# Where unit 30 spreads its inverses: ahead of, or behind, a marker in SyncE's queue

## The chip, the cores and the metric

The kernel runs on one core of a Trainium2 chip. The metric is the device time of one execution in microseconds (us), as the median of several runs; lower is better.

## The reference

Multi-query attention with 32 heads and a gated feed-forward part are computed from the same 2048 x 512 input, and mixed row by row by a gate:

```
g = sigmoid((x * gate_w).sum(-1, keepdims=True))
q = (x @ wq) in 32 heads of 16;   k = x @ wk;   v = x @ wv
p = softmax(q k^T * 16 ** -0.5);  a = (p v, heads side by side) @ wo
b = (sigmoid(x @ w_gate) * (x @ w_up)) @ w_down
out = g * a + (1 - g) * b
```

All of it is float32. F is 1792.

## The kernel before

The queries stand in 4 blocks of 512 rows (b), the heads in 8 groups of 4, so attention has 32 units, u = 0 to 31. For each unit TensorE first makes scores to find each row's maximum (L1141, reduced by VectorE at L1143), then makes the scores again with the maxima taken off (L1150), ScalarE takes their exponentials (L1152, tiles `p`), and TensorE multiplies these by the values (L1008, "V" here: 4 matmuls for each of 16 chunks of keys). `v_aug` has a column of ones, so the sums of the softmax come out of the same matmuls. Between these stand the matmuls of the feed-forward part and of the output projection (`fill`, L1115). They use 64 of the 128 rows each, so two of them, or one and a score matmul, run side by side in the two halves.

A matmul pair of `fill` changes halves in the middle of a job: what half 0 has begun in a bank, half 1 goes on with. For this the kernel puts an empty instruction, a marker, in SyncE's queue (L1119). It waits for the last matmul of the first half, and the first matmul of the other half on that bank waits for the marker (`CROSS`, L1117).

SyncE also issues every DMA, all in one queue and in program order. So an instruction of SyncE that waits holds up all DMAs behind it.

What a unit needs at its end goes through these steps. `finish` (L1015) and `add_sums` (L1022) bring the values of the unit together in tile `ou`. `store` sends the sums to DRAM tile `sd` (L1030) and all of `ou` to `od` (L1031). `sums` reads the sums back in another shape into `rc` (L1036). `invert` takes the reciprocals on VectorE (L1045). `send_inverse` writes them to DRAM tile `rd` (L1049). `spread` reads `rd` back into `bc`, each row repeated over the 16 rows of its head (L1055). `divide` on GpSimd multiplies `vd` by `bc` (L1063) and splits the product into a high and a low part, tile `o` (L755 and L756). `o` is an operand of the output projection.

Units go by twos through `vd`, `bc` and `o`, with one exception. Unit 30, the last but one, does not wait for unit 31: its heads are put into both halves of `vd` and `bc`, so that its `spread` issues four DMAs, `bc`, `vd`, `bc`, `vd` (L1055, L1057, L1055, L1057). Its projection is a job of its own, "e" (matmuls `bank<-we,o`, 12 of them), which lies among the scores and values of unit 31. Unit 31 itself is finished by other code at the end of the kernel (L1177 to L1208).

The order of all work is fixed beforehand. TensorE's order is a string written out by hand (`ORDER`, one character a step). The steps of the other engines are put between by a small planner (`State`), which keeps an estimated time, in a unit of its own, for each engine: `self.now` for TensorE, `self.sp` for SyncE's queue, `self.dma` for transfers. An event is put on a list with an estimated time (`after`, L181) and is written into the program at the first step of TensorE whose estimated time is not earlier (`tick`, L280). `send` and `issue` (L169, L175) advance `self.sp` by the cost of issuing and return an estimate of when the data has landed. At the end each engine's instructions are chained in that program order. The estimates set only the order; on the chip semaphores decide when something runs.

Of the kernel before, what the change touches and what calls it, by code (L numbers as in the profile page):

```python
# [26 lines left out]
NU = NB * NG  # L27
# [30 lines left out]
ISSUE, SMALL, TEN_KB, LAST, SAFE, SURE = 185, 750, 20, 300, 300, 150  # L58
# [64 lines left out]
class State:  # L123
# [170 lines left out]
    def event(self, what, args):  # L294
        self.acts.append((what, *args))
        if what == "load_x":
            self.x_loaded[args[0]] = self.send(KC, 1024)
        elif what == "store_q":
            at = self.send(2, 512)
            self.q_ready[tuple(args)] = at  # L300
            self.ba_release(("query", *args), at)
        elif what == "send_max":
            self.after(self.issue(SEND_SQUARE, 16) + SAFE, "place_max", *args)
        elif what == "max_square":
            self.after(self.on("dve", self.now, SQUARE) + TAIL, "send_max", *args)
        elif what == "place_max":
            self.max_ready[args[0]] = self.issue(PLACE, 16) + 150
        elif what == "store":
            at = self.sums_free[args[0] % OU] = self.issue(470, 264) + SAFE
            self.after(at, "sums", *args)  # L310
        elif what == "sums":
            self.after(self.issue(430, 136) + 2 * SAFE, "invert", *args)
        elif what == "invert":
            self.after(self.on("dve", self.now, INVERSE), "send_inverse", *args)
        elif what == "send_inverse":
            self.after(self.send(1, 8) + SAFE, "spread", *args)
        elif what == "spread":
            u = args[0]
            at = self.issue(250, 128)
            if u % 2 or u == NU - 2:  # L320
                self.task(2, at + 2 * SAFE, "divide", u)
        elif what == "out":
            self.tile_free[self.tile_of[tuple(args)]] = self.send(1, 256)
# [933 lines left out]
```

## Time and profile before

| What | us |
|---|---|
| Median of 3 runs (1583.82 to 1584.93) | 1583.95 |
| The profiled execution, its own time | 1582.52 |
| Span of its profile, first to last instruction | 1580.7 |
| TensorE matmuls (PE) busy | 1567.2 (99%) |
| VectorE (DVE) busy | 1338.9 (85%) |
| ScalarE (ACT) busy | 1232.2 (78%) |
| GpSimd (POOL) busy | 803.8 (51%) |
| DMA, mean over the span | 65 GB/s |

PE is TensorE's matmuls, PEld its loading of weights, and SPq is SyncE's queue with its DMA issues. Times of single rows count from the start of the span. A row of the timeline gives the start, the duration, the engine, the line, the operation with output and inputs, how many instructions were merged into the row, and in brackets how long the engine stood idle before it and what ended that. Matmuls of the two halves overlap, so the busy times of single lines add up to more than the time that passes.

### The profile page before, as it was taken

The numbers are of one execution on the slowest core, as the hardware profiler recorded it, in microseconds if no ns is written. First come the engines' busy times: TensorE is split into PE (matmuls) and PEld (weight loads), VectorE is DVE, ScalarE is ACT, GpSimd is POOL, SyncE is SP. The second block draws the span as 40 slices with busy tenths as digits, with TensorE's granted clock in tenths as the row PEclk, the third lists the DMA queues.
The fourth block names the chain that finished last, engine by engine and source line by source line (L and its number), as shares of the span: only waits on it lengthen the run. The fifth ranks groups of instructions, "written<-read, shape, count | busy, mean of one in ns | idle before, by whom it ended". The sixth has DMA issues, their size and how long they took to land.

```text
span 1580.7 us, 33642 instructions
## 1 busy us (share of the span) xinstructions
PE 1567.2 (99%) x12910; PEld 1009.0 (64%) x12910; DVE 1338.9 (85%) x2277; ACT 1232.2 (78%) x2429; POOL 803.8 (51%) x727
## 2 busy tenths in 40 slices
PE   9999999999999999999999999999999999999997
PEld 7766666666666666666666666667675666656653
DVE  6899899988898888889798888888889888988841
ACT  4277878788788787878788777878878887878895
POOL 4353472655574164367475346275547517357351
PEclk9999999999999999999999999999999999999999
DMA  7421120222122121122122212021213202111011
GB/s 245 169 88 51 35 86 16 66 62 83 43 83 66 36 79 53 35 76 71 45 83 63 64 49 78 18 67 60 77 46 92 65 23 87 46 40 59 18 53 40
DMA packets 63076, 103.43 MB, mean 65 GB/s; under 512 B 24530, under 2 KB 24786, under 8 KB 62916
## 3 DMA queue, kind: packets, MB, share of 16 engines
q1 hardware_dynamic: 62916, 101.29, 20.5%
q8 instruction: 101, 1.65, 0.4%
q14 instruction: 59, 0.48, 0.1%
HBM read 79.51 MB, written 21.75 MB: 64 GB/s over the span
## 4 chain that ended last, share of the span: by engine, by line
PE 96%; DVE 1%; DMA 1%; SPq 1%; ACT 0%; issue 0%; POOL 0%; DVEq 0%; ACTq 0%; POOLq 0%
PE bank L1115 32%; PE bank L1008 29%; PE bank L1141 17%; PE bank L1150 16%; PE bank L853 2%; DVE mx L1143 1%; DMA vd<-od 0%; DMA wqr<-wq 0%; SPq L968 0%; DVE q L948 0%; DMA qs<-qd 0%; ACT x L780 0%; PE bank L1196 0%; DVE x L786 0%; SPq L765 0%
## 5 line engine op out<-in xcount | busy, mean ns | idle before, releaser
L1143 DVE TENSOR_REDUCE mx<-bank 128x1 f32<-128x512 f32 x2048 | 1253.7, 680 | 168.7 <-PE bank L1141 104.0
L1152 ACT ACTIVATE p<-bank 128x512 f32<-128x512 f32 x2048 | 1040.2, 664 | 10.9 <-PE bank L1150 7.7
L1150 PE MATMUL bank<-qs,ks 64*128 64x512 f32 x2048 | 723.7, 399 | 0.0
L1141 PE MATMUL bank<-ks,qs 64*128 64x512 f32 x2048 | 684.2, 404 | 0.5 <-DMA qs<-qd 0.5
L1008 PE MATMUL bank<-p,v_aug 128*32 128x512 f32 x4096 | 480.6, 597 | 0.0
L1141 PEld LDWEIGHTS bank<-ks,qs 64*128 64x128 f32 x2048 | 339.8, 184 | 138.7 <-issue 56.5
L1150 PEld LDWEIGHTS bank<-qs,ks 64*128 64x128 f32 x2048 | 359.6, 184 | 91.3 <-ACT p L1152 27.8
L1015 ACT COPY ou<-bank 128x512 f32<-128x512 f32 x205 | 125.0, 610 | 272.3 <-PE bank L1008 124.1
L1022 POOL TENSOR_TENSOR ou<-ou,ou 128x512 f32<-128x512 f32 x174 | 224.3, 1289 | 170.2 <-ACT ou L1015 167.7
L1115 PE MATMUL bank<-wd,hl 64*128 64x512 f32 x1344 | 272.7, 391 | 0.0
L1115 PE MATMUL bank<-x,wu 64*128 64x512 f32 x1344 | 271.3, 390 | 0.6 <-SPq L1119 0.4
L1008 PEld LDWEIGHTS bank<-p,v_aug 128*32 128x32 f32 x4096 | 113.1, 109 | 248.4 <-issue 220.5
L1115 PE MATMUL bank<-x,wg 64*128 64x512 f32 x1344 | 271.2, 391 | 0.0
L1115 PEld LDWEIGHTS bank<-wd,hl 64*128 64x128 f32 x1344 | 199.8, 184 | 20.6 <-issue 2.5
L1115 PEld LDWEIGHTS bank<-x,wg 64*128 64x128 f32 x1344 | 200.8, 184 | 17.5 <-issue 1.2
L1115 PEld LDWEIGHTS bank<-x,wu 64*128 64x128 f32 x1344 | 201.1, 184 | 17.0 <-issue 2.5
L1094 POOL TENSOR_TENSOR ba<-ba,pa_d 128x512 f32<-128x512 f32 x35 | 44.5, 1283 | 93.2 <-ACT pa_d L1091 93.1
L829 POOL CAST wg<-rg 128x1024 fp32r<-128x1024 f32 x27 | 28.0, 1039 | 123.8 <-PE bank L1115 63.9
L829 POOL CAST wu<-ru 128x1024 fp32r<-128x1024 f32 x27 | 28.1, 1040 | 95.8 <-PE bank L1115 93.2
L756 POOL TENSOR_TENSOR wd<-rd,wd 128x512 fp32r<-128x512 f32 x56 | 72.3, 1292 | 4.5
L756 POOL TENSOR_TENSOR hl<-h,hl 128x512 fp32r<-128x512 f32 x56 | 72.0, 1286 | 4.5
L1115 PE MATMUL bank<-wa,o 64*128 64x512 f32 x360 | 70.4, 391 | 0.0
(80 smaller groups left out, 747.2 us busy)
## 6 DMA issues: line engine op xcount, KB each, us to landing
rg<-wg SPq DMA_DIRECT2D x28, 512.0 KB
ru<-wu SPq DMA_DIRECT2D x28, 512.0 KB
rd<-wd SPq DMA_DIRECT2D x28, 512.0 KB
qs<-qd SPq DMA_DIRECT2D x192, 64.0 KB
qd<-q SPq DMA_DIRECT2D x32, 256.0 KB
od<-ou SPq DMA_DIRECT2D x31, 256.0 KB
xf<-x_in SPq DMA_DIRECT2D x16, 256.0 KB
vd<-od SPq DMA_DIRECT2D x32, 128.0 KB
```

The lines of the kernel that those rows point to most:

```text
L756: lo.tensor_tensor(hl[:, 1, :], raw, f32(hl[:, 0, :]), op=ALU.subtract)
L829: nc.gpsimd.tensor_copy(WS[item][:, 0, :], raw)
L853: nc.tensor.matmul(ps, w[:, p, part(kc)], X[b, kc][:, q, :], start=i == 0, stop=i == 3 * KC - 1)
L1008: nc.tensor.matmul(ps[32 * j:32 * j + 32, :], v_aug[:, c, :], PT.pop((u, c, j)), start=start, stop=stop)
L1015: nc.scalar.copy(to, ps)
L1022: nc.gpsimd.tensor_tensor(SUMS[u], SUMS[u], PARTS_OF[u].pop(0), op=ALU.add)
L1094: nc.gpsimd.tensor_tensor(BA[b, t], BA[b, t], PA[b, t].pop(0), op=ALU.add)
L1115: ins = nc.tensor.matmul(banks[i], l, r, start=start, stop=stop)
L1141: nc.tensor.matmul(banks[i], qs_t[u % 3][r, pr, part(qt)], ks[r, kb * 512:(kb + 1) * 512], start=True, stop=True)
L1143: nc.vector.tensor_reduce(MX[u][:, pr, h, qt, kb:kb + 1], banks[i], axis=AX.X, op=ALU.max)
L1150: nc.tensor.matmul(banks[i], ks[r, part(c)], qs_t[u % 3][r, pr, :], start=True, stop=True)
L1152: nc.scalar.activation(p, banks[i], AF.Exp, scale=0.25)
```

## The change

One event of the planner is due at another time. Before, `spread` was put on the list for the moment at which `send_inverse` is estimated to have landed, plus a margin (`SAFE`). Now, for unit 30 alone, it is put there for the moment at which SyncE is estimated to have issued `send_inverse`. The other units keep their order.

```diff
         elif what == "send_inverse":
-            self.after(self.send(1, 8) + SAFE, "spread", *args)
+            at = self.send(1, 8) + SAFE
+            self.after(self.sp if args[0] == NU - 2 else at, "spread", *args)
         elif what == "spread":
             u = args[0]
             at = self.issue(250, 128)
             if u % 2 or u == NU - 2:
                 self.task(2, at + 2 * SAFE, "divide", u)
```

The changed file has one line more, so lines behind it carry a number greater by one (L1055 is L1056 there). In the rows below the tiles of unit 30 are `sd_20058`, `od_20059`, `rc_20107`, `rd_20150`, `bc_20057` and `vd_20056`; a marker has no row of its own, and shows in the waits of the SyncE instruction behind it (`PE_49`) and of the TensorE matmul that needs it (`SP_sequencer_49`).

SyncE's queue from the sending of the sums of unit 30 to the end, before:

```order
L1030 DMA sd_20058<-ou_19636 4x512 [waits PE_49,DMAHW4_49,Pool_49]
L1031 DMA od_20059<-ou_19636 128x512
L1036 DMA rc_20107<-sd_20058 128x16 [waits DMAHW6_49,DMAHW4_49]
L1049 DMA rd_20150<-rc_20107 128x16 [waits DMAHW7_49,DVE_49]
L1055 DMA bc_20057<-rd_20150 64x1x512 [waits PE_49,DMAHW7_49,DMAHW0_49]
L1057 DMA vd_20056<-od_20059 64x1x512 [waits DMAHW5_49]
L1055 DMA bc_20057<-rd_20150 64x1x512 [waits DMAHW2_49]
L1057 DMA vd_20056<-od_20059 64x1x512 [waits DMAHW3_49]
L1207 DMA out<-ba_0_16676 128x512 [waits PE_49,DVE_49]
```

The same place now:

```order
L1031 DMA sd_20058<-ou_19636 4x512 [waits PE_49,DMAHW4_49,Pool_49]
L1032 DMA od_20059<-ou_19636 128x512
L1037 DMA rc_20107<-sd_20058 128x16 [waits DMAHW6_49,DMAHW4_49]
L1050 DMA rd_20150<-rc_20107 128x16 [waits DMAHW7_49,DVE_49]
L1056 DMA bc_20057<-rd_20150 64x1x512 [waits DMAHW7_49,DMAHW0_49]
L1058 DMA vd_20056<-od_20059 64x1x512 [waits DMAHW5_49]
L1056 DMA bc_20057<-rd_20150 64x1x512 [waits DMAHW2_49]
L1058 DMA vd_20056<-od_20059 64x1x512 [waits DMAHW3_49]
L1208 DMA out<-ba_0_16676 128x512 [waits PE_49,DVE_49]
```

The DMAs stand in the same order. What moved is a marker: before, the marker of the last "a" job's first half on bank 7 stood between `rd` and the first `bc`, and is the `PE_49` of that `bc`. Now it stands behind the four DMAs of `spread`, beside the marker of bank 2, which stood there already.

On TensorE the two matmuls that need these markers, on bank_79 (bank 7) and bank_74 (bank 2), stand among scores of unit 31, before:

```order
L1115 MATMUL bank_74<-wa_1_0_19890,o_19717 128x512
L1150 MATMUL bank_72<-qs_108,ks 128x512 [waits Activation_49]
L1115 MATMUL bank_79<-wa_0_0_19783,o_17409 128x512 [waits SP_sequencer_49]
L1150 MATMUL bank_76<-qs_108,ks 128x512 [waits Activation_49]
L1115 MATMUL bank_79<-wa_0_0_19783,o_17409 128x512
L1150 MATMUL bank_78<-qs_108,ks 128x512 [waits Activation_49]
L1115 MATMUL bank_79<-wa_0_0_19783,o_17409 128x512
L1150 MATMUL bank_75<-qs_108,ks 128x512 [waits Activation_49]
L1115 MATMUL bank_79<-wa_0_1_19786,o_18682 128x512
L1115 MATMUL bank_74<-wa_0_0_19783,o_17409 128x512 [waits SP_sequencer_49]
```

Nothing moved there: these rows and all others of TensorE, VectorE, ScalarE and GpSimd stand in the same order in the changed kernel. The first use of `o` of unit 30 (tile `o_20240`), 24 rows further on in TensorE's order, before:

```order
L1008 MATMUL bank_77<-p_8_1_1_20170,v_aug 32x512
L1150 MATMUL bank_73<-qs_108,ks 128x512 [waits Activation_49]
L1115 MATMUL bank_79<-we_0_0_19958,o_20240 128x512 [waits DVE_49,Pool_49]
L1115 MATMUL bank_72<-we_0_0_19958,o_20240 128x512 [waits Activation_49]
L1115 MATMUL bank_79<-we_0_0_19958,o_20240 128x512
L1115 MATMUL bank_72<-we_0_0_19958,o_20240 128x512
L1115 MATMUL bank_79<-we_0_0_19958,o_20240 128x512 [waits Pool_49]
L1150 MATMUL bank_76<-qs_108,ks 128x512 [waits Activation_49]
```

Here too the order is the same now, and so are the waits; only the numbers that tiles get in program order differ (`o_20240` is `o_20200`). The first of these five "e" matmuls waits for the high part of `o`, the fifth for the low part.

## The prediction

> **What bounds the kernel now.** I read the page first (engines, chain), then the chain in order of time near the end, then SyncE's waits and the timelines of SyncE, GpSimd, TensorE and ScalarE around unit 30's `spread`.
>
> ```profile
> PE 1567.2 (99%) x12910; PEld 1009.0 (64%) x12910; DVE 1338.9 (85%) x2277; ACT 1232.2 (78%) x2429; POOL 803.8 (51%) x727
> PE 96%; DVE 1%; DMA 1%; SPq 1%; ACT 0%; issue 0%; POOL 0%; DVEq 0%; ACTq 0%; POOLq 0%
> ```
>
> TensorE is busy for 99% of the span and carries 96% of the chain. Only where the chain leaves TensorE can the order of another queue be worth anything. Near the end it does:
>
> ```profile
> 1547.13 0.26 PE bank L1150
> 1547.47 0.07 issue
> 1547.60 0.57 SPq L1055
> 1548.16 0.05 issue
> 1548.22 0.55 SPq L1057
> 1548.81 0.51 SPq L1055
> 1549.36 6.18 DMA vd<-od
> 1555.60 0.09 issue
> 1555.69 1.27 POOL vd L1063
> ```
>
> Read from below: `divide` waited for the last of the four transfers of `spread`, that one for SyncE's issue, and the first issue (1547.60) for a matmul of TensorE that ended just before. A transfer between DRAM tiles and `bc` has no business waiting for a matmul; the waits of SyncE between 1530 and 1560 us tell what it was:
>
> ```profile
> SPq L1119 <- PE bank L1115: 13.4, 3, 6.9
> ```
>
> Columns: total, times, longest. L1119 is the marker. SyncE stood 6.9 us at one marker with `spread` queued behind it. The issues on both sides of it:
>
> ```profile
> 1540.24 0.32 SPq L1049 DMA_DIRECT2D rd<-rc  x1
> 1547.60 0.57 SPq L1055 DMA_DIRECT2D bc<-rd  x1
> ```
>
> What the delay costs TensorE stands in its timeline, with GpSimd's beside it:
>
> ```profile
> 1553.81 0.49 PE L1150 MATMUL bank<-qs,ks 64*128 64x512 f32 x1
> 1557.68 2.14 PE L1115 MATMUL bank<-we,o 64*128 64x512 f32 x5 [3.38 <-POOL o L755]
> ```
> ```profile
> 1555.69 1.26 POOL L1063 TENSOR_TENSOR vd<-vd,bc 128x512 f32<-128x512 f32 x1 [19.77 <-DMA vd<-od]
> 1557.02 0.61 POOL L755 CAST o<-vd 128x512 fp32r<-128x512 f32 x1
> 1557.71 1.27 POOL L756 TENSOR_TENSOR o<-vd,o 128x512 fp32r<-128x512 f32 x1
> ```
>
> TensorE is through with its earlier work at 1554.30 (1553.81 + 0.49) and stands for 3.38 us until the high part of `o` is there. GpSimd had been idle for 19.77 us and is no limit.
>
> **What the change does, step by step.** It adds and removes no instruction. The four issues of `spread` pass one marker. The first still has to wait until `rd` has landed. Where no marker lies between the two, the trace has that time:
>
> ```profile
> 1503.02 0.31 SPq L1049 DMA_DIRECT2D rd<-rc  x1
> 1504.43 0.56 SPq L1055 DMA_DIRECT2D bc<-rd  x1
> ```
>
> 1.41 us from issue to issue. So the first `bc` is issued at 1540.24 + 1.41 = 1541.65 instead of 1547.60, **5.95 us earlier**. From there I move the whole piece rigidly: the four issues and the landing take 1555.54 - 1547.60 = 7.94 us (chain above: 1549.36 + 6.18), and no other transfer is in the way, since DMA is at rest between the landing of `rd` and the first `bc`:
>
> ```profile
> 1541.00:1541.50 0.50, 0.50 (x8) 0.00 (x0) 0.00 (x0) 0.50 (x2) 0.00 (x0) 1.00 0.18 17
> 1541.50:1542.00 0.50, 0.50 (x8) 0.42 (x6) 0.00 (x0) 0.50 (x2) 0.00 (x0) 1.00 0.00 0
> 1547.00:1547.50 0.50, 0.50 (x8) 0.23 (x10) 0.00 (x0) 0.50 (x2) 0.00 (x0) 1.00 0.00 0
> ```
>
> (The last three columns are the granted clock, DMA share and GB/s; the ten slices between the second and the third row show 0.00 as well.) `divide` then starts at 1549.74, the high part of `o` is ready at 1551.68 and the low part at 1553.03. TensorE asks for the high part at 1554.30 and for the low part about 0.4 us later. The cover is 2.6 us and 1.7 us, so **the stall goes whole**, even if the landing were 1.5 us slower than I took it.
>
> The marker itself now comes after the four issues. They occupy SyncE from 1541.65 for 2.27 us (1547.60 to 1549.36 + 0.51), to 1543.92, and the matmul for which the marker waits ends only at about 1547.4. So the marker is not later than before and costs nothing. Nothing else stands in SyncE's queue there until the outputs.
>
> What is gained is more than the stall, because TensorE's clock fell in it. The rows are stretches of TensorE's work, with matmuls in brackets and the granted clock behind:
>
> ```profile
> 1549.17:1552.82 3.65, 3.65 (x35) 1.00 0.25 86
> 1552.82:1553.81 0.99, 0.99 (x10) 1.00 0.33 120
> 1554.30:1557.68 3.38, 0.00 (x1) 0.74 0.04 14
> 1557.68:1561.46 3.78, 3.65 (x13) 0.50 0.00 0
> 1561.46:1563.06 1.60, 1.60 (x9) 0.60 0.00 0
> 1563.06:1563.95 0.89, 0.89 (x10) 1.00 0.00 0
> 1570.79:1580.70 9.91, 3.25 (x39) 0.95 0.28 106
> ```
>
> - The stall: 3.38 us.
> - The 13 matmuls of 1557.68 to 1561.46 (9 "e", 4 scores) ran at clock 0.50, and the fifth waited for the low part. The stretch that begins at 1549.17 is the same mix at full clock; its 35 records count the five that reach in from neighbouring V groups, so about 30 in 3.65 us, 0.122 us each. 13 of them are 1.58 us: 3.78 - 1.58 = 2.20 us.
> - The V group of 1561.46 to 1563.06: the same group at full clock took 0.99 us, so 0.61 us.
> - From 1563.06 on the clock was back, and nothing changes.
>
> The sum is 3.38 + 2.20 + 0.61 = 6.19 us. The Trainium skill, "TensorE: Matmul & The Clock Gate", section "Part 1: The HAM clock gate", says that an idle window of about 3.4 us halves TensorE's clock, and that about 3.4 us of work release it. The trace agrees in kind: 0.50 after the pause, full from 1563.06. By that rule alone, a TensorE that no longer pauses keeps its clock, and the sum is the same.
>
> What is late next is ScalarE, which must deliver the last 16 exponentials before the last V group:
>
> ```profile
> 1549.74 5.50 ACT L1152 ACTIVATE p<-bank 128x512 f32<-128x512 f32 x11 [0.45 <-PE bank L1150]
> 1559.90 2.06 ACT L1152 ACTIVATE p<-bank 128x512 f32<-128x512 f32 x4 [4.67 <-PE bank L1150]
> 1563.59 5.99 ACT L1152 ACTIVATE p<-bank 128x512 f32<-128x512 f32 x12 [1.63 <-PE bank L1150]
> ```
>
> At 5.99 / 12 = 0.50 us each, without a gap from 1555.24 on, they are done at 1563.2. Before, 1.21 us lay from the last exponential (1569.58) to TensorE's end of the values (1570.79), so ScalarE allows 1564.4. By TensorE's sum it is 1570.79 - 6.19 = 1564.6. The two nearly coincide, and scores need banks that ScalarE and VectorE have to empty first. That can only cost: from nothing to the 1.2 us that one V group and a bank's release take. I take 0.1 us, the nearer end, since both engines have room on average. The last 9.91 us (transposes, last projection, outputs) move along unchanged.
>
> So the gain is **6.1 us**. Against the profiled execution's 1582.52 us that is 1576.4. That execution lies 1.4 us below the median of the runs, 1583.95, against which the result will stand: 1583.95 - 6.1 = **1577.8 us**.
>
> **The rivals.**
>
> *The clock falls anyway.* Without the stall TensorE runs into ScalarE's pace, and pauses in pieces for banks. If these pieces lowered the clock, the 13 matmuls and the V group would keep their 3.78 and 1.60 us, and only the stall would go: 1583.95 - 3.4 = 1580.6. Against it: over the whole span the clock is 0.998, with ScalarE emptying banks all along. The Trainium skill, same page, section "A second HAM failure mode: psum-queue depth-cycling", tells of a kernel in which short idle pieces between groups of matmuls did make the clock swing; in this trace no run of such pieces shows it.
>
> *ScalarE and VectorE become the bound.* Each piece of waiting for a bank adds up to 1.2 us as above: about 1579.0. For it: the two sums are only 0.2 us apart.
>
> *No change.* The first `bc` also waits for an earlier transfer's slot, or `rd` lands as late as the marker came (7.36 us instead of 1.41): 1583.9. Against it: nothing was in flight after 1541.5, and the longest wait of SyncE for `rd` in the whole trace is short:
>
> ```profile
> SPq L1055 <- DMA rd<-rc: 22.2, 20, 2.8
> ```
>
> *Slower: TensorE waits for the marker behind `spread`.* Before, the marker waited only for its matmul; now it waits also for `rd` to land and for four issues. TensorE needs it in the "a" job at about 1549.7, 5.8 us after the four issues end in my reckoning. So it decides from 1.41 + 5.8 = 7.2 us of landing on, and then each us costs one. With a landing of twice the slowest seen above, 12.4 us, the issues end at 1554.9: TensorE stands 5.2 us there and the stall at "e" remains, 1589.1. Against it: the same 2.8 us.
>
> **How the numbers follow.** 0.2%, about what a measurement of this kernel can tell from no change, is 3.2 us. The forecast, 1577.8, gets 0.76; the clock rival (1580.6, on the edge of 0.2%) 0.07, half to each side; ScalarE and VectorE as the bound (1579.0) 0.09; no change 0.05; slower 0.03. Faster: 0.76 + 0.09 + 0.035, so 0.88; the same: 0.035 + 0.05, so 0.09; slower 0.03. The range reaches up to the clock rival, 1580.6, and down to 1576.5: the sum of 6.19 and the quarter us by which the first "e" matmul could start before the score ahead of it has ended, with the 1 us by which the runs of before differ.
>
> **What would show it.** Right: the first `bc` of unit 30 issued about 1.4 us after `rd`, no marker's wait between; `divide` near 1549.7; no idle before `bank<-we,o`; the granted clock 1.00 from 1554 to 1564; the last V groups ending near 1564.7 and a span near 1574.6. Wrong: a wait of TensorE for L1119 near 1549; a clock of 0.5 in spite of no stall; gaps of 0.3 us and more before scores that name ScalarE or VectorE; or `bc` issued early while `divide` still starts after 1552, which would mean that the transfers, and not their issue, were late.

## The result and the profile after

| | median us | runs |
|---|---|---|
| Kernel before | 1584.44 | 4 (1583.82 to 1586.09) |
| Changed kernel | 1576.30 | 4 (1575.21 to 1578.34) |

The ratio is 0.9953, with a 95% interval of 0.9940 to 0.9966. The change makes the kernel faster by about 7.4 us (5.4 to 9.5). A second comparison, five runs of the changed kernel beside fresh runs of before, gave 0.9963 (0.9950 to 0.9977), 5.9 us. The profiled execution took 1578.34 us, its span is 1576.6 us.

The page's first line and the chain:

```profile
PE 1566.5 (99%) x12910; PEld 1013.5 (64%) x12910; DVE 1339.9 (85%) x2277; ACT 1232.1 (78%) x2429; POOL 803.3 (51%) x727
PE 97%; DVE 1%; ACT 0%; SPq 0%; DMA 0%; POOL 0%; issue 0%; DVEq 0%; POOLq 0%; ACTq 0%
```

The work is the same; the chain's share outside TensorE has shrunk. SyncE's waits between 1530 and 1560 us (total, times, longest), and its issues around `spread`:

```profile
SPq L1120 <- PE bank L1116: 9.5, 3, 5.9
SPq L1056 <- DMA rd<-rc: 1.1, 1, 1.1
```
```profile
1542.53 0.32 SPq L1050 DMA_DIRECT2D rd<-rc  x1
1543.98 0.57 SPq L1056 DMA_DIRECT2D bc<-rd  x1
...
1545.75 0.51 SPq L1058 DMA_DIRECT2D vd<-od  x1
```

The first `bc` follows `rd` after 1.45 us instead of 7.36, held only by the landing of `rd`. The marker that moved is still waited for, but now the four issues are ahead of it. The 5.9 us above belong to another marker, ahead of the sending of the sums; from 1547 to 1550 us SyncE's waits are these:

```profile
SPq L1120 <- PE bank L1116: 3.4, 1, 3.4
```

GpSimd and TensorE:

```profile
1551.83 1.30 POOL L1064 TENSOR_TENSOR vd<-vd,bc 128x512 f32<-128x512 f32 x1 [13.64 <-DMA vd<-od]
1553.19 0.61 POOL L756 CAST o<-vd 128x512 fp32r<-128x512 f32 x1
1553.88 1.30 POOL L757 TENSOR_TENSOR o<-vd,o 128x512 fp32r<-128x512 f32 x1
```
```profile
1555.07 1.07 PE L1009 MATMUL bank<-p,v_aug 128*32 128x512 f32 x8
1556.07 0.50 PE L1151 MATMUL bank<-qs,ks 64*128 64x512 f32 x1
1556.07 0.96 PE L1116 MATMUL bank<-we,o 64*128 64x512 f32 x5
...
1557.98 1.06 PE L1009 MATMUL bank<-p,v_aug 128*32 128x512 f32 x8
...
1563.08 3.64 PE L1009 MATMUL bank<-p,v_aug 128*32 128x512 f32 x32
```

No bracket stands behind the five "e" matmuls: TensorE did not wait. The clock in these stretches (last three columns: granted clock, DMA share, GB/s):

```profile
1555.07:1557.98 2.91, 2.91 (x24) 1.00 0.03 6
1557.98:1558.98 1.00, 1.00 (x11) 1.00 0.00 0
1558.98:1566.72 7.74, 7.74 (x67) 1.00 0.00 0
```

To compare runs whose first microseconds differ, I take one stretch of TensorE: from the start of the V group of chunk 8 of unit 31 (1552.82 before, 1555.07 here) to the end of the last V group (1570.79 and 1566.72). It took 17.97 us before and takes **11.65 us** now, 6.32 less. The spans differ by only 4.1 us, since the stretch begins 2.25 us later here, which has to do with the first microseconds of the span (last section).

### The profile page after: what moved, and what is told of

The parts are those of the page before. It is cut to its first block, busy times and chain, and to the rows that moved or that the text cites. A ratio compares the mean times of both kernels' runs of the same rounds, so it can differ in the third digit from the quotient of the medians.

```text
span 1576.6 us, 33642 instructions
## 1 busy us (share of the span) xinstructions
PE 1566.5 (99%) x12910; PEld 1013.5 (64%) x12910; DVE 1339.9 (85%) x2277; ACT 1232.1 (78%) x2429; POOL 803.3 (51%) x727
## 4 chain that ended last, share of the span: by engine, by line
PE 97%; DVE 1%; ACT 0%; SPq 0%; DMA 0%; POOL 0%; issue 0%; DVEq 0%; POOLq 0%; ACTq 0%
PE bank L1116 32%; PE bank L1009 30%; PE bank L1142 17%; PE bank L1151 16%; PE bank L854 3%; DVE mx L1144 0%; SPq L969 0%; DMA qs<-qd 0%; ACT x L781 0%; PE bank L1197 0%; DMA wkv_raw<-wkv 0%; DVE x L787 0%; POOL wkv_s L757 0%; DVE q L949 0%; DVE wkv_stack L887 0%
## 5 line engine op out<-in xcount | busy, mean ns | idle before, releaser
L1116 PEld LDWEIGHTS bank<-x,wu 64*128 64x128 f32 x1344 | 201.2, 184 | 16.5 <-issue 2.5
L1116 PEld LDWEIGHTS bank<-x,wg 64*128 64x128 f32 x1344 | 201.1, 184 | 16.3 <-issue 1.2
```

Source lines behind the costliest of these rows:

```text
L1116: ins = nc.tensor.matmul(banks[i], l, r, start=start, stop=stop)
```

## The experiments

In this table "low part" is the time from the start of that V group to the end of the low part of `o` (L756 on GpSimd), "lateness" is what it lies beyond 1.50 us, and "clock" is what remains of the stretch beyond 11.65 us and the lateness. All are worked out from rows like those above. The 1.50 us comes from the first repetition (12.37 - 11.65 = 0.72; 2.22 - 0.72 = 1.50); the other rows test it. The three e2 runs and the two e6 runs are one profiled execution each.

| Run | low part | lateness | stretch | clock |
|---|---|---|---|---|
| before | 6.16 | 4.66 | 17.97 | 1.66 |
| before, e6_before_a | 6.37 | 4.87 | 17.43 | 0.91 |
| before, e6_before_b | 7.55 | 6.05 | 18.99 | 1.29 |
| change | 0.11 | 0 | 11.65 | 0 |
| change, e0_again | 2.22 | 0.72 | 12.37 | 0 |
| e1_marker_gpsimd | 0.86 | 0 | 11.64 | 0 |
| e3_busy_stall | 6.31 | 4.81 | 16.43 | 0 |
| e2_late1 | 2.23 | 0.73 | 12.38 | 0 |
| e2_late3 | 4.77 | 3.27 | 16.49 | 1.57 |
| e2_late4 | 6.15 | 4.65 | 19.15 | 2.85 |
| e4_all_units | 0.08 | 0 | 11.65 | 0 |
| e5_vd_early | 0.95 | 0 | 11.67 | 0 |

**The change again (e0_again).**

> The changed kernel once more, beside fresh runs of the kernel before. The stretch from the V group of chunk 8 of unit 31 to the end of the values is 17.97 us before and 11.65 us in the profile of the change. Theory (the whole gain is in that stretch): ratio 1 - 6.3 / 1584.4 = 0.9960, stretch 11.6 to 11.8 us, and the rest of the 8.1 us between the medians is scatter of the first 14 us of the span. Rival (something outside the stretch gains as well): ratio 0.995 or less again.

Measured: ratio 0.9963 (0.9950 to 0.9977), so the theory's 0.9960 lies in the middle, though the interval just reaches the rival's 0.995. The stretch was longer than expected, and the profile shows why:

```profile
1542.24 0.57 SPq L1056 DMA_DIRECT2D bc<-rd  x1
```
```profile
1551.65 1.29 POOL L1064 TENSOR_TENSOR vd<-vd,bc 128x512 f32<-128x512 f32 x1 [15.84 <-DMA vd<-od]
```
```profile
1555.03 0.50 PE L1116 MATMUL bank<-we,o 64*128 64x512 f32 x1 [0.32 <-POOL o L757]
```

From the first `bc` to `divide` it took 9.41 us here, and 7.85 in the first profile of the change. The fifth "e" matmul then waited for the low part. So the transfers of `spread` scatter (7.85 to 9.48 us over the runs with all four together). Besides, `rd` went out later against TensorE: 11.96 us ahead of the V group of chunk 8 here, 12.54 in the first profile of the change, because the read of the sums into `rc` took longer (`rd` 3.21 us behind its issue, against 2.56). The cover is thinner than one profile tells.

**The marker through another queue (e1_marker_gpsimd).** The kernel before; `spread` stays where it was, and only the one marker leaves SyncE's queue.

```diff
-            CROSS[j.key, x] = nc.sync.nop()
+            queue = nc.gpsimd if (j.key, h) == (("a", NB - 1, 1), 1) else nc.sync
+            CROSS[j.key, x] = queue.nop()
```

> The kernel before, with spread where it was; only the one marker ahead of it goes through GpSimd's queue, which is idle there, instead of SyncE's. Theory (the marker in SyncE's queue is all that held spread up): bc issued 1.4 us after rd, no idle time ahead of the e matmuls, stretch 11.6 to 11.9 us, ratio as for the change, about 0.996. Rival (the gain needs spread's new place in program order, or came from the order of something else): stretch 17 to 18 us, ratio 1.000.

```profile
1541.36 0.32 SPq L1049 DMA_DIRECT2D rd<-rc  x1
1542.81 0.57 SPq L1055 DMA_DIRECT2D bc<-rd  x1
```
```profile
1553.51 1.06 PE L1008 MATMUL bank<-p,v_aug 128*32 128x512 f32 x8
1554.50 0.96 PE L1115 MATMUL bank<-we,o 64*128 64x512 f32 x5
...
1561.51 3.64 PE L1008 MATMUL bank<-p,v_aug 128*32 128x512 f32 x32
```

`bc` 1.45 us behind `rd`, no wait, stretch 11.64 us, ratio 0.9959 (0.9946 to 0.9971). With `spread` in its old place the whole gain is there: the marker ahead of it in SyncE's queue was the cause, and the rival falls.

**The stall kept, the clock kept up (e3_busy_stall).** The kernel before, with 13 matmuls ahead of the first "e" matmul, on a bank that "e" overwrites.

```diff
+        if j.kind == "e" and not BUSY:
+            BUSY.append(i)
+            for _ in range(13):
+                nc.tensor.matmul(banks[i], ks[:, :P], ks[:, :512], start=True, stop=True)
         ins = nc.tensor.matmul(banks[i], l, r, start=start, stop=stop)
```

> The kernel before with the stall kept, but TensorE kept busy in it: 13 matmuls of 128 rows whose result is overwritten stand ahead of the first e matmul. What the stall itself costs stays; what the halved clock behind it costs goes. Theory (clock): granted clock 1.00 throughout, the first e matmul where it was (4.9 us after the V group of chunk 8 begins), stretch 16.0 to 16.3 us instead of 17.97, total 1.8 us shorter, ratio 0.9989. Rival (the slow matmuls behind the stall come from late operands, not from the clock): stretch 17.8 to 18.1 us.

```profile
1554.16 3.24 PE L1118 MATMUL bank<-ks 128*128 128x512 f32 x13
1557.74 0.73 PE L1119 MATMUL bank<-we,o 64*128 64x512 f32 x4 [0.34 <-POOL o L755]
1559.10 0.50 PE L1119 MATMUL bank<-we,o 64*128 64x512 f32 x1 [0.62 <-POOL o L756]
```
```profile
1557.74:1560.43 2.69, 2.07 (x14) 1.00 0.00 0
```

The operand is as late as before, the clock is 1.00 instead of 0.50 (the first row's 13 filling matmuls held it up), and the stretch is 16.43 us, a little above the theory's 16.3 and far from the rival's 17.8. Ratio 0.9988 (0.9979 to 0.9997): beside the first profile of before, keeping the clock up took 1.5 us off the stretch. 11.65 plus the lateness of 4.81 gives 16.46, so the stretch's formula holds far from where its constant was taken.

**How much lateness costs (e2_late1, e2_late3, e2_late4).** The changed kernel with one, three or four products more on GpSimd ahead of `divide`, into a part of `o` that is written again.

```diff
+        for _ in range(3 if u == NU - 2 else 0):
+            nc.gpsimd.tensor_tensor(o[:, 1, :], vd, bc, op=ALU.mult)
         nc.gpsimd.tensor_tensor(vd, vd, bc, op=ALU.mult)
```

> The changed kernel with one more product of 1.29 us on GpSimd (overwritten afterwards) between the landing of spread's transfers and divide. The high part of o is ready about 2.5 us ahead of TensorE in the change, the low part 1.5 us ahead. Theory (the cover is real): no idle time, stretch 11.6 to 11.9 us. Rival (TensorE already waits for the low part in the change): stretch 12.9 us.

> As before with three such products, 3.87 us. The high part comes 1.1 us after TensorE is through with its earlier work, the low part 2.3 us after the fifth e matmul could run. Theory A (a short pause costs its length, the clock stays): granted clock 1.00, stretch 11.65 + 2.3 = 13.9 us. Theory B (any pause halves the clock): clock 0.5 behind it, stretch 15.5 to 16 us.

> As before with four such products, 5.16 us: idle time of 2.4 us ahead of the first e matmul, the low part 3.6 us late. Theory A (the clock stays up to a pause of this length): stretch 15.3 us. Theory B (it is halved): 16.5 to 17.2 us.

One product already made the fifth "e" matmul wait 0.34 us; the stretch was 12.38 us, between theory and rival. The cover was there in the change's first profile (1.4 us). It is used up by the product, which took 1.37 us with its gap, and by transfers that landed 0.77 us later against TensorE. Three products, TensorE and its clock:

```profile
1555.94 0.73 PE L1118 MATMUL bank<-we,o 64*128 64x512 f32 x4 [1.99 <-POOL o L756]
1557.30 0.75 PE L1118 MATMUL bank<-we,o 64*128 64x512 f32 x1 [0.62 <-POOL o L757]
```
```profile
1552.47:1555.94 3.47, 1.49 (x11) 1.00 0.02 5
1555.94:1559.69 3.75, 3.13 (x14) 0.69 0.00 0
1559.69:1562.10 2.41, 2.41 (x16) 0.77 0.00 0
1562.10:1568.96 6.86, 6.86 (x59) 1.00 0.00 0
```

The four matmuls behind the pause of 1.99 us still took 0.73 us, as at full clock in e3_busy_stall. Read in windows of 0.02 us, the clock falls only at 1557.37, just behind the second pause of 0.62 us. Theory A falls all the same, also with four products (pauses of 3.37 and 0.62 us), where the clock drops at 1558.49, in the second pause:

```profile
1557.58:1561.36 3.78, 3.16 (x14) 0.62 0.00 0
1561.36:1564.80 3.44, 3.44 (x16) 0.50 0.00 0
1564.80:1571.87 7.07, 7.07 (x59) 0.96 0.00 0
```

But theory B, as a fixed price, does not hold either: the stretches, 16.49 and 19.15 us, are longer than its 15.5 to 16 and 16.5 to 17.2. The clock cost 1.57 us with the pause of 1.99 and 2.85 with that of 3.37, where the kernel before paid 1.66 after nearly the same pause (3.38).

**The kernel before, profiled twice more (e6_before_a, e6_before_b).**

> The kernel before, profiled again, for the scatter of the stretch. The low part comes 6.2 us after the V group of chunk 8 begins, 4.7 us late. Theory (stretch = 11.65 us + lateness of the low part + what the halved clock costs, and the last depends on where the pause falls): stretch 17.5 to 19.3 us, the clock's share 1.3 to 3 us and different from run to run. Rival (the clock's share is fixed): 17.9 to 18.1 us again.

> The kernel before a third time, with the same expectations: 17.5 to 19.3 us if the clock's share varies, 17.9 to 18.1 us if it is fixed.

```profile
1557.90 2.15 PE L1115 MATMUL bank<-we,o 64*128 64x512 f32 x5 [3.59 <-POOL o L755]
```
```profile
1559.95 2.15 PE L1115 MATMUL bank<-we,o 64*128 64x512 f32 x5 [4.77 <-POOL o L755]
```

17.43 and 18.99 us, so the share varies. The first is just under the expected 17.5, and the shares, 0.91 and 1.29 us, lie below the expected 1.3 to 3. The longest pause of all, 4.77 us in the second, cost 1.29 us of clock, less than the pause of 1.99 us above: the length does not set the price.

What does is in the same traces. In this table "idle from" is the end of TensorE's last matmul before the pause, and "half clock" the time in which the granted clock was 0.50, read in windows of 0.02 us. "Work at half" is the part of it that lies behind the end of the low part of `o`, and "clock" is the column of the table above.

| Run | idle from | half clock | length | work at half | clock |
|---|---|---|---|---|---|
| before | 1554.30 | 1555.91 to 1562.73 | 6.82 | 3.75 | 1.66 |
| e6_before_a | 1554.31 | 1557.85 to 1561.26 | 3.41 | 2.06 | 0.91 |
| e6_before_b | 1555.18 | 1557.38 to 1564.21 | 6.83 | 2.97 | 1.29 |
| e2_late3 | 1553.95 | 1557.37 to 1560.78 | 3.41 | 3.41 | 1.57 |
| e2_late4 | 1554.21 | 1558.49 to 1565.31 | 6.82 | 6.44 | 2.85 |

The half clock lasted 3.41 us or twice that, whatever the pause, and in each of the twelve profiles all recorded changes of the clock lie whole multiples of 3.413 us apart. The loss is 0.43 to 0.46 of the work at half. So the price depends on where the pause lies on this grid of 3.41 us, and on how much work then runs before the clock returns. A pause of 1.99 us in e4_all_units (below) even left the clock at 1.00, where e2_late3 lost it with pauses of 1.99 and 0.62 us:

```profile
1334.46:1336.45 1.99, 0.00 (x1) 1.00 0.37 144
1336.45:1340.00 3.55, 3.55 (x31) 1.00 0.02 5
```

The Trainium skill, "TensorE: Matmul & The Clock Gate", section "Part 1: The HAM clock gate", describes a free-running window of about 3.4 us over which activity is judged; the step of 3.41 us in these rows agrees with it. That the half rate comes after at least one idle window of that length does not fit, if idle means without work: in the kernel before the clock fell 1.61 us after the last matmul, and in e2_late3 0.81 us of matmuls lay in the 3.42 us ahead of the fall. How much standing in a window is enough, no run here was made to find.

**The change for all units (e4_all_units).**

```diff
-            self.after(self.sp if args[0] == NU - 2 else at, "spread", *args)
+            self.after(self.sp, "spread", *args)
```

> The change made for all units instead of unit 30 alone. Theory (only unit 30 has a consumer that waits; for the others TensorE never stood for o): the tail as in the change, the rest the same, ratio to the kernel before 0.995 to 0.998, so within 0.1% of the change. Rival (SyncE now waits for the landing of rd, 1.4 us in each unit, ahead of loads that are needed): new idle time of GpSimd on the loads of weights or of TensorE on scores, total 2 to 20 us longer than the change.

Ratio 0.9979 (0.9970 to 0.9988), median 1580.77 of 11 runs against 1577.72 for the change on the same chip. The intervals of the two ratios overlap a little, but on that chip the five runs of the change took 1576.73 to 1578.84 us and the eleven of this kernel 1578.50 to 1581.93: only one of the five is slower than the fastest of the eleven. So a loss of about 3 us against the change is shown; the theory's 0.1%, 1.6 us, is too little, and the rival's 2 to 20 us holds. The stretch is 11.65 us as in the change; what is lost lies ahead of it. One such place, SyncE's queue and TensorE:

```profile
1325.70 0.32 SPq L1050 DMA_DIRECT2D rd<-rc  x1
1329.21 0.56 SPq L1056 DMA_DIRECT2D bc<-rd  x1
1329.83 0.45 SPq L749 DMA_DIRECT2D ru<-wu  x1
1330.33 0.60 SPq L994 DMA_DIRECT2D md<-sq  x1
...
1334.65 1.68 SPq L1002 DMA_DIRECT2D qs<-md  x2
```
```profile
1336.45 0.50 PE L1116 MATMUL bank<-x,wu 64*128 64x512 f32 x1 [1.99 <-SPq L1120]
```

`bc` waits for `rd` with a load of weights (`ru`) behind it. That load goes out at 1329.83, next to the maxima (`md`) that follow; in the change it went out 2.14 us ahead of `bc`. The chain there names `md`, 4.25 us in landing, then the two `qs` issues that wait for it, then a marker behind these, and TensorE stands 1.99 us at the marker. SyncE's wait for `rd` over the whole run is 44.3 us in 31 waits, double the 22.2 in 20 of before. Where the remaining 1 us goes was not traced.

**The two `vd` transfers earlier (e5_vd_early).** In the changed kernel they are issued with `sums`, ahead of `rd`.

> The change, and besides the two vd transfers of unit 30 are issued with sums, ahead of rd, instead of between the two bc. Behind rd only the two bc transfers are left. Theory (the low part of o is on the edge: where it comes later than 1.5 us after the V group of chunk 8 begins, each us costs one): divide starts 2 to 3.5 us earlier than in the change, no idle time ahead of the fifth e matmul, stretch 11.6 to 11.7 us, total 0 to 0.7 us below the change, ratio 0.996. Rival (the early vd transfers hold up rd, whose landing bc waits for): bc issued 3 us and more behind rd, the low part as late as before, stretch 12.4 us or more.

```profile
1540.79 0.45 SPq L1051 DMA_DIRECT2D rd<-rc  x1
1545.30 1.09 SPq L1057 DMA_DIRECT2D bc<-rd  x2
```
```profile
1550.37 1.30 POOL L1062 TENSOR_TENSOR vd<-vd,bc 128x512 f32<-128x512 f32 x1 [14.46 <-DMA bc<-rd]
```

Both sides were partly right. `rd` was held up by the `vd` transfers: `bc` came 4.51 us behind it instead of 1.45. The two `bc` alone then took 5.07 us. From `rd` to `divide` that is 9.58 us, against 9.30 and 10.86 in the two profiles of the change: no gain beyond the scatter. The stretch, 11.67 us, and the ratio 0.9957 (0.9943 to 0.9970) do not tell it from the change, whose median was 1577.72 on its chip and this one's 1576.06. Nothing faster than the change was shown.

## Why the prediction was right, step by step

**The marker as the cause, and the move of 5.95 us.** Right. `bc` follows `rd` after 1.45 us where 1.41 was taken, and e1_marker_gpsimd shows that nothing but the marker held it.

**The marker itself costs nothing behind the four issues.** Right here: SyncE was through with them at 1546.26 (1545.75 + 0.51) and waited for TensorE, not the other way round. What the rival "slower" feared, TensorE waiting for a marker that stands behind DMA issues, happened in e4_all_units, in another place: 1.99 us.

**The stall goes whole.** Right in the first profile. The claim that it would even if the landing were 1.5 us slower was wrong. In e0_again `divide` began 9.41 us after the first `bc`, 1.32 us more than the 8.09 us (1555.69 - 1547.60) of the trace from which I took the landing, and `rd` went out 0.6 us later; 0.32 us of waiting for the low part came back and the stretch was 0.72 us longer. Two sizes were wrong. I took the transfers' 7.94 us from one execution as if it were fixed. And I counted the cover of the low part from 1554.7, where the runs put the last harmless moment 1.50 us after the start of the V group, at 1554.32: the cover was 1.3 us, not 1.7.

**The sum, 6.19 us.** The stretch got 6.32 us shorter. Of the two ways to divide it, the runs support this one: 4.66 us because the low part was late and 1.66 us for the clock. My "slow" terms (2.20 + 0.61) put the wait for the low part, 1.3 us, and the clock together; e3_busy_stall separates them. All terms come from one execution. In the three profiles of the kernel before the stall was 3.38, 3.59 and 4.77 us and the clock's loss 1.66, 0.91 and 1.29 us, so that 6.19 came so near to the 6.32 of one pair of profiles is in part luck.

**ScalarE as the next bound, 0.1 us.** Not contradicted, and not tested. With the operand in time, ScalarE ran without a gap (1552.00 to 1565.50) and TensorE's stretch had no idle time. Which of the two sets the 11.65 us no run separates, and a term of 0.1 us is smaller than what the profiles differ by.

```profile
1552.00 13.50 ACT L1153 ACTIVATE p<-bank 128x512 f32<-128x512 f32 x27 [0.45 <-PE bank L1151]
```

**The clock rival** did not happen: 1.00 throughout, with ScalarE at its limit.

**The total.** 1576.3 us measured, 1577.8 predicted; the measured median lies just under the lower end of the stated range, 1576.5. Of the 8.1 us between the medians 6.3 are shown in the stretch. Over all profiles the stretch averages 18.13 us in the kernel before (three) and 12.01 us in the changed one (two), 6.1 apart, and the second comparison of times gave 5.9 us. The rest I put to scatter: the kernel before has stretches of 17.43 to 18.99 us and runs of 1581.8 to 1586.55. That another place gained too is not shown by any row, and not excluded below 1 us or so.

## What to carry to other kernels

An empty instruction that only passes a semaphore on is a real place in an in-order queue: put on the queue that issues DMAs, it makes every transfer behind it wait for the compute that it watches. So look at what stands between a transfer's operand and its issue, and move the marker or the transfer, but only where a consumer waits: where none does, the early issue makes the queue wait for its operand and pushes other loads back. Price a pause of TensorE as its length plus a clock loss that is not fixed: 0.9 to 2.9 us in these runs, a little under half of the time in which work went on at half clock. And take the length of a transfer from several executions before calling something covered.

## What the runs showed of the hardware that was not expected

The start of the span scatters by up to 2.6 us, with the same instructions. The same nine matmuls, before and after:

```profile
7.34 2.33 PE L853 MATMUL bank<-x,wkv_s 128*128 128x512 f32 x9
```
```profile
7.92 3.58 PE L854 MATMUL bank<-x,wkv_s 128*128 128x512 f32 x9
```

In the first profile of the change they took 3.58 us, where the other profiled runs have 2.31 to 2.57. The clock column prints 1.00 there in both, but that is no measurement: in the kept traces the records of the clock begin only later, with a change to full clock, at 10.66 us of the span in the first profile of the change, at 6.26 us in that of before, and at 4.26 to 5.42 us in the ten others. In the first profile of the change the matmuls that start from 8.49 to 9.77 us take 0.63 us each, as long as matmuls under a recorded clock of 0.50 in e2_late3; those from 10.88 us on take 0.39. So TensorE ran at half clock about 4.4 us longer there. Half speed from 6.62 to 10.66 us costs about 2.0 us, by estimate, which is most of the 2.25 us by which the stretch begins later in that profile (1555.07, against 1552.47 to 1552.83 in several others). That run, 1578.34 us, is also the slowest of the four of the changed kernel. A single profiled span is a poor measure of a change of 6 us.
